# Attention backward on one core: how head rows lie in DRAM, and who turns the dS tiles

## The chip, the cores and the metric

The kernel runs on one core of a Trainium2 chip. A core has five engines that run their own instruction streams and meet through semaphores: TensorE (PE, matrix products; PEld is its weight load), VectorE (DVE), ScalarE (ACT), GpSimd (POOL) and SyncE (SP), which here does nothing but issue DMAs. ScalarE and GpSimd issue some DMAs too. SBUF is the on-chip memory with 128 partitions, PSUM takes the products of TensorE, DRAM lies outside. The metric is device time in microseconds (us), the median of several runs.

## What is computed

The reference is one transformer block with conditional layer norm, its output, and the gradients of nine inputs:

```python
h = _layernorm(x) * (1 + ca) + sa
x = x + ga * _A_ref(h, A_wqkv, A_wo)            # attention, 32 heads of 16, sequence 2048, width 512
h = _layernorm(x) * (1 + cb) + sb
x = x + gb * _B_ref(h, B_w1, B_b1, B_w2, B_b2)  # dense 512 -> 1792, squared relu, 1792 -> 512
...
_out, _vjp = jax.vjp(_f, A_x, A_wqkv, A_wo, B_w1, B_b1, B_w2, B_b2, c, w_mod)
_grads = _vjp(grad_out)
```

The change touches the attention. Forward, for each head: scores = q k^T / 4, p = softmax(scores), o = p v. Backward, with dO the gradient of o: dP = dO v^T, dS = p * (dP - delta), where delta is the row sum of dO * o; then dq = dS k, dk = dS^T q, dv = p^T dO. dS lies with queries on the partitions; dq needs it with keys there, so every tile of dS has to be turned (transposed).

## The kernel before

The program has five parts in time: preparation (layer norm, the first products, to about 42 us), the forward attention with the dense parts of three of the four query chunks woven in (42 to 1006), the last dense chunk (1006 to 1124), the attention backward (1124 to 2390), and the remaining gradients (2390 to 2514).

**Head rows.** A matmul of one head contracts over 16 rows, and TensorE's tiles have 32. Four heads make a group of 128 rows, HG = 8 groups: head h of a group has partitions 32h to 32h+31. Rows 0 to 15 of these are its data (q, k, v or dO, turned so that the sequence runs along the row). Row 16 holds one side of a bound or correction: ones for k and v, the row's negative bound on the score (`m_st`) for q, and -delta (`d_st`) for dO; thereby one product gives score minus bound, or dP minus delta. The other 15 rows are zeros (q, dO) or ones (k, v), which contribute nothing. In DRAM only the data rows are kept (`qkT_st`, `vT_st`, `dOT_st`), with `m_st` and `d_st` beside them. `row_loads` (L131) loads a group tile as four DMAs of 16 rows, one for each head, and a fifth for the bound's rows; the spare rows were filled once, by memsets (L979, L980, `head_fill` L1201, L1505, L1506) and by `copy_const` on ScalarE (L1232).

**Forward.** Units of 128 keys run through (query chunk, group, key tile). `fload` (L544) loads a group's k and q through SyncE, 16 units ahead, into two buffers each: nine DMAs. A unit has four score products (L560), two exponentials of ScalarE over 128x1024 (`ET`, L562), and four products with v (L576).

**Backward.** The loop goes through 512 units: group hg, key chunk kc (512 keys), query chunk qc, query tile qi; four units with the same chunks are a batch, and there are 128 batches. In a unit:
- `score` (L1595): four products, one for each head, 128 queries x 512 keys, into one of three PSUM banks; `expo` (L1601): four exponentials on ScalarE into E_u (four buffers).
- `dp_pair` (L1615): two products into psD_u (two buffers), and one VectorE product dS_u = psD_u * E_u over 128x1024 (L1617); twice a unit. Two units share one dS_u tile; there are four such tiles.
- `k_quad` (L1655) and `v_quad` (L1664): products for dk and dv.
- `transpose_unit` (L1624 on): after each second unit SyncE issues one DMA that turns both units' dS (1 MB, L1632) into dsT (three buffers, one a batch).
- `dq_quad` (L1682): two batches later, products of dsT with k into the dq accumulator; `dq_out` copies them out on ScalarE (L1695) and adds on GpSimd (L1700).

In odd batches (`on_pe`, L1620) the last unit is turned otherwise: unit 2 alone by a DMA of 0.5 MB (L1630), unit 3 by 16 transposes on TensorE (`pe_turn`, L1645) with two copies out of PSUM on ScalarE (L1761). TensorE's order of work within a batch is written out by hand as a string of tokens: s a score, e an exponential, D a dp_pair, q a quad, t a turn on TensorE, T its copy, d half of dq's products, Q their way out, f a filler matmul that keeps TensorE busy. `order_t` holds the turns and four fillers, `order_n` neither:

```python
toks, bank = order_t if on_pe(b - 1) else order_n
```

Between batches, ScalarE's queue issues the next group's loads (`plan_head`, L1579, through `load`, L1577): four loads of q in its other layout, 4 + 5 + 4 + 5 of k, q, v and dO, one every four D tokens. It also stores the results of dk and dv four times a group (a quarter each, L1667 on) and those of dq four times a group.

**Queues.** Every DMA issued by SyncE stands in one queue in program order; an instruction there that waits or takes long holds up the ones behind it. The order of all engines in these parts is the program's.

Of the kernel before, what the change touches and what calls it, by code (L numbers as in the profile page):

```python
# [17 lines left out]
BF = dt.bfloat16  # L18
# [16 lines left out]
def kernel(  # L35
# [55 lines left out]
    qkT_st = dram.tile([2, D, n], BF, name="qkT_st")  # L91
    vT_st = dram.tile([D, n], BF, name="vT_st")
    dOT_st = dram.tile([D, n], BF, name="dOT_st")
    m_st = dram.tile([H, n], BF, name="m_st")
    d_st = dram.tile([H, n], BF, name="d_st")
# [35 lines left out]
    def row_loads(dst, srcT, hg, cols, aux=None):  # L131
        for h in range(4):
            i = hg * 4 + h
            yield dst[32 * h:32 * h + DH, :], srcT[i * DH:(i + 1) * DH, cols]
        if aux is not None:
            yield dst.rearrange("(h c) n -> c h n", h=4)[DH], aux[hg * 4:(hg + 1) * 4, cols]

    def load_rows(*args):
        for to, fro in row_loads(*args):
            SP.dma_start(out=to, in_=fro)  # L140
# [6 lines left out]
    with ExitStack() as ph:  # L147
# [385 lines left out]
        def store_grad(c, lag, dOT, dlt, more=3):  # L533
            dltT = wk.tile([P, P], BF, name="dltT", tag="dltT", bufs=1)
            later(lag, sp, dltT[:], dlt.rearrange("p t h -> p (t h)"), True)
            cols = slice(512 * c, 512 * c + 512)
            later(lag + more, sp, dOT_st.rearrange("(b p) n -> p b n", p=P)[:, :, cols], dOT.rearrange("p b t q -> p b (t q)"))
            for ti in range(4):
                later(lag + more, sp, d_st[:, 512 * c + ti * P:512 * c + (ti + 1) * P], dltT[H * ti:H * ti + H, :])
# [4 lines left out]
        def fload(qc, hg):  # L544
            i = hg % 2
            kt_sb, qt_sb = kts[i], qts[i]
            load_rows(kt_sb, qkT_st[1], hg, slice(0, n))
            load_rows(qt_sb, qkT_st[0], hg, slice(512 * qc, 512 * qc + 512), m_st)
            fh[qc, hg] = (qt_sb, kt_sb)
# [115 lines left out]
        def later_stage(i):  # L665
            if i < 4:
                vT = tmpT[:, 4 * (i % 2):4 * (i % 2) + 4, :].rearrange("p a q -> p (a q)")
                sp(vT[:, 0:n], v_st[:, i * P:(i + 1) * P], True)
                later(3, sp, vT_st[i * P:(i + 1) * P, :], vT[:, 0:n])
                return  # L670
# [79 lines left out]
        qkT_v = qkT_st.rearrange("a (b p) n -> p a b n", p=P)  # L750
# [64 lines left out]
        def value_tile(t, acc):  # L815
            for ic in range(DC):
                PE.matmul(acc, h1Ts[t // 4][:, ic, (t % 4) * P:(t % 4 + 1) * P], wqkv[:, ic, 2 * D:3 * D],
                          start=(ic == 0), stop=(ic == DC - 1))
            if t % 4 == 0:
                psp["v"] = cb.tile([P, 4, D], BF, name="vP", tag=("a_c", "xn2_c")[t // 4 % 2])  # L820
            vt = psp["v"][:, t % 4, :]
            DVE.tensor_copy(vt, acc)
            DVE.tensor_copy(vaug[:, t, 0:H, 0:DH], vt.rearrange("p (h d) -> p h d", d=DH))
            if t % 4 == 3:
                later(1, sp, v_st.rearrange("(t p) d -> p t d", p=P)[:, t - 3:t + 1, :], psp["v"][:])
# [10 lines left out]
        def mod_rows(j):  # L836
            pm = mm()
            for ic in range(DC):
                PE.matmul(pm[:], sbcT[:, ic, :], wmod_slice(j)[:, ic, :], start=(ic == 0), stop=(ic == DC - 1))
            if j in (1, 4):  # L840
                DVE.tensor_scalar(modbc[:, j, :], pm[:], 1.0, None, ALU.add)
            else:
                DVE.tensor_copy(modbc[:, j, :], pm[:])

        def prep():
# [28 lines left out]
            DVE.tensor_reduce(onecol, identb.rearrange("p (h c) -> p c h", c=32)[:, DH, :], AX.X, ALU.add)  # L874
            POOL.memset(sel0, 0.0)
# [84 lines left out]
            sp(qkT_st[1, 0:P, :], KTs[0][:])  # L960
            sp(qkT_st[0, 0:P, 0:512], sP[:, 4, :])
# [13 lines left out]
            for k in range(2):  # L975
                sp(m_st[4 * k:4 * k + 4, 0:512], mrow.rearrange("(h c) n -> c h n", h=4)[DH + k])
            for t in range(4):
                value_tile(t, acc4()[:])
            POOL.memset(kts[1][:], 1.0)  # L979
            POOL.memset(qts[1][:], 0.0)  # L980
# [3 lines left out]
            run_due(True)  # L984
# [3 lines left out]
        def plan_tasks():  # L988
# [5 lines left out]
            def key_tile(b, g):  # L994
# [8 lines left out]
                if g == QC - 1:  # L1003
                    later(1, sp, qkT_st[1, b * P:(b + 1) * P, :], KTs[b][:])
# [6 lines left out]
            def query_tile(g, hb):  # L1011
# [7 lines left out]
                if g == 0:  # L1019
                    later(1, sp, qkT_st[0, hb * P:(hb + 1) * P, 0:512], sP[:, lo + hb, :])  # L1020
                elif hb == 3:
                    later(1, sp, qkT_v[:, 0, :, chunk_cols(g)], sP[:, lo:lo + 4, :])
# [10 lines left out]
            def bound(g, hbs):  # L1033
# [10 lines left out]
                later(1, sp, m_st[h0:h1, chunk_cols(g)], mrow[h0:h1, :])  # L1044
# [156 lines left out]
        def head_fill(i):  # L1201
            for key in ("k", "v", "q", "do"):
                POOL.memset(hsets[i][key][:], 1.0 if key in ("k", "v") else 0.0)

        def kvq_loads(hg):
            hs = hsets[hg % 2]
            for i in range(4):
                yield hs["qs"][:, 4 * i:4 * i + 4, :], q_st[hg][:, 4 * i:4 * i + 4, :]
            yield from row_loads(hs["k"], qkT_st[1], hg, slice(0, n))
            yield from row_loads(hs["q"], qkT_st[0], hg, slice(0, n), m_st)  # L1210
            yield from row_loads(hs["v"], vT_st, hg, slice(0, n))
# [22 lines left out]
        def last_chunk(O_c, L, w1T, w2T):  # L1234
# [76 lines left out]
            later(17, copy_const, hsets[0]["v"][:], 1.0)  # L1311
# [109 lines left out]
            def grad(ti):  # L1421
                attn_grad(c, ti, daT, woT, dOs_c, O_c, dlt)
                ACT.activation(dpad[:, ti, :, 0:DH], dOs_c[:, ti, 0:4 * DH].rearrange("p (h d) -> p h d", d=DH), AF.Identity)
                ACT.activation(dpad[:, ti, :, DH:DH + 1], dlt[:, ti, 0:4].unsqueeze(2), AF.Identity)
# [69 lines left out]
        with ExitStack() as ph2:  # L1494
            pools["mm"] = ph2.enter_context(tc.tile_pool(name="psM2", bufs=4, space=bass.MemoryType.PSUM))
            with tc.manual_schedule(engines={PE.engine, ACT.engine, DVE.engine, SP.engine, POOL.engine}):
# [8 lines left out]
                DVE.memset(hsets[0]["q"][:], 0.0)  # L1505
                DVE.memset(hsets[0]["do"][:], 0.0)  # L1506
                copy_const(hsets[0]["k"][:], 1.0)
# [17 lines left out]
                def head_loads():  # L1525
                    done = slice(0, 512 * (QC - 1))
                    for i, (to, fro) in enumerate(list(kvq_loads(0)) + list(row_loads(hsets[0]["do"][:, done], dOT_st, 0, done, d_st))):
                        later(i, sp, to, fro)
# [20 lines left out]
    with ExitStack() as ph:  # L1549
# [29 lines left out]
        def plan_head(hg):  # L1579
            j0 = (hg - 1) * 128 + 14  # L1580
            loads = list(kvq_loads(hg)) + list(row_loads(hsets[hg % 2]["do"], dOT_st, hg, slice(0, n), d_st))
            for i, (to, fro) in enumerate(loads):
                at(j0 + 4 * i, load, to, fro)
# [37 lines left out]
        def on_pe(b):  # L1621
            return b % 2 == 1
# [35 lines left out]
        def v_quad(u):  # L1658
# [7 lines left out]
            if qt == TT - 1:  # L1666
# [3 lines left out]
                else:  # L1670
                    part = slice(kc * 512, (kc + 1) * 512)
                    at(cur["j"] + 4, load, dVKtP[hg][:, part], hst[hg]["vk"][:, part])
# [12 lines left out]
        def dq_out(b):  # L1685
# [15 lines left out]
            if kc == QC - 1 and qc == QC - 1 and hg < HG - 1:  # L1701
                for hq in range(4):
                    r = hg % 2 * 64 + hq * DH
                    at(cur["j"] + 6 + hq, load, dQc[hg // 2, r:r + DH, :], st["dq"][32 * hq:32 * hq + DH, :])
# [16 lines left out]
        with tc.manual_schedule(engines={PE.engine, ACT.engine, DVE.engine, SP.engine, POOL.engine}):  # L1721
            head_fill(1)
# [329 lines left out]
```

## Time and profile before

| what | us |
|---|---|
| runs: median (all) | 2519.93 (2519.93, 2520.61, 2513.72) |
| profiled execution: span from first to last instruction | 2513.8 |
| busy: TensorE, ScalarE, VectorE, GpSimd | 2335.0, 2302.6, 1809.7, 348.0 |
| 41 to 1006: busy TensorE, ScalarE, VectorE (of 965) | 862.1, 942.4, 454.2 |
| 1006 to 1124: the same (of 118) | 111.9, 53.3, 79.6 |
| 1124 to 2390: the same (of 1266) | 1212.4, 1228.4, 1186.2 |
| 2390 to 2514: the same (of 124) | 117.5, 50.3, 62.3 |
| mean granted TensorE clock, whole span | 0.982 |

The profiled execution took as long as the fastest of the three runs, so sums that start from its span are compared with runs that spread by 7 us (0.3%). Rows of a group give the busy time of all its instructions, the mean duration of one in ns, and the idle time of the engine just before them with what ended most of it. Durations of consecutive instructions overlap on ScalarE and VectorE, so start to start is shorter than the mean duration. SyncE has no busy row: its instructions only issue, and appear as SPq with a start and a duration.

### The profile page before, as it was taken

To read this page: it belongs to the slowest core of one execution; us is meant where nothing else is said; L and a number is where in the kernel's file an instruction comes from. 1 tells how busy PE (TensorE), PEld (TensorE's weight loads), DVE (VectorE), ACT (ScalarE), POOL (GpSimd) and SP (SyncE) were. 2 spreads that over 40 slices of the span, in tenths; PEclk is the share of its full clock that TensorE was granted. 3 is DMA by queue.
4 is the path that set the end of the run, shared out by engine and by line. 5 is a ranking of instruction groups with operands and counts; after the bars stand their busy time and mean duration, and the time that the engine had idled before them with its cause. 6 is when DMAs were issued, how large, how long until landed. Compare 5 with 4: busy or idle time off the path is not lost.

```text
span 2513.8 us, 49777 instructions
## 1 busy us (share of the span) xinstructions
PE 2335.0 (93%) x18916; PEld 777.9 (31%) x19005; DVE 1809.7 (72%) x2317; ACT 2302.6 (92%) x3577; POOL 348.0 (14%) x370
## 2 busy tenths in 40 slices
PE   7898889989988998999999999999999999999999
PEld 3232223222322323442233322233222323222343
DVE  6555153455435454579999999999998999999872
ACT  7999999999999999539999999999999999999952
POOL 2000000210333142210111101011010110110100
PEclk9999999999999999999999999999999999999999
DMA  6476465356748765969999999999999999999972
GB/s 203 129 193 177 136 131 139 96 160 136 110 88 174 153 131 118 264 211 184 207 203 210 199 198 204 204 201 206 204 200 206 199 195 204 206 199 215 197 254 72
DMA packets 1220981, 447.15 MB, mean 178 GB/s; under 512 B 1096951, under 2 KB 1191607, under 8 KB 1220486
## 3 DMA queue, kind: packets, MB, share of 16 engines
q1 hardware_dynamic: 1192822, 409.11, 81.8%
q0 software_dynamic: 10944, 16.78, 4.5%
q10 hardware_dynamic: 16976, 18.07, 2.8%
q8 instruction: 149, 2.44, 0.4%
q14 instruction: 90, 0.74, 0.1%
HBM read 96.75 MB, written 73.95 MB: 68 GB/s over the span
## 4 chain that ended last, share of the span: by engine, by line
PE 40%; ACT 39%; issue 7%; DVE 7%; DMA 4%; SPq 2%; ACTq 1%; POOL 0%; DVEq 0%; another core or an unknown queue 0%
ACT E_u L1601 24%; ACT ET L562 11%; PE dqacc L1682 5%; PE psST L560 4%; PE psS_A L1595 3%; PE pm L233 3%; PE accVK L1655 2%; ACT dsT L1761 2%; PE oacc L576 2%; PE psS_B L1595 2%; SPq L178 2%; PE psS_C L1595 2%; PE pm L412 2%; PE pdh L1876 2%; PE pwq L1910 2%
## 5 line engine op out<-in xcount | busy, mean ns | idle before, releaser
L1617 DVE TENSOR_TENSOR dS_u<-psD_u,E_u 128x1024 bf16<-128x1024 f32 x1024 | 1186.2, 1219 | 71.2 <-PE psD_u L1615 25.5
L562 ACT ACTIVATE ET<-psST 128x1024 bf16<-128x1024 f32 x1024 | 942.3, 1247 | 25.3 <-PE psST L560 24.7
L1601 ACT ACTIVATE E_u<-psS_A 128x512 bf16<-128x512 f32 x768 | 509.6, 664 | 11.0 <-PE psS_C L1595 8.5
L1601 ACT ACTIVATE E_u<-psS_B 128x512 bf16<-128x512 f32 x768 | 502.6, 654 | 12.5 <-PE psD_u L1615 3.4
L1615 PE MATMUL psD_u<-iv,ido 32*128 32x512 bf16 x2048 | 409.9, 388 | 0.5 <-DVE dS_u L1617 0.2
L560 PE MATMUL psST<-qt_sb,kt_sb 32*128 32x512 bf16 x2048 | 316.5, 387 | 53.0 <-ACT ET L562 46.2
L1601 ACT ACTIVATE E_u<-psS_C 128x512 bf16<-128x512 f32 x512 | 333.7, 652 | 2.7 <-PE psS_B L1595 1.0
L1595 PE MATMUL psS_B<-ik,iq 32*128 32x512 bf16 x768 | 294.9, 384 | 12.5 <-ACT E_u L1601 5.0
L1595 PE MATMUL psS_A<-ik,iq 32*128 32x512 bf16 x768 | 293.4, 382 | 11.1 <-DVE dwlast L237 1.0
L1595 PEld LDWEIGHTS <-iq 32*128 32x128 bf16 x2048 | 130.5, 91 | 316.0 <-issue 299.9
L1655 PE MATMUL accVK<-dS_u,qz 128*32 128x512 bf16 x2048 | 213.0, 390 | 0.5 <-PE psD_u L1615 0.3
L576 PE MATMUL oacc<-ET,vaug 128*32 128x512 bf16 x2048 | 207.8, 396 | 1.9 <-DVE ostage L580 1.9
L1664 PE MATMUL accVK<-E_u,dOs_tok 128*16 128x512 bf16 x2048 | 203.7, 386 | 0.0
L1700 POOL TENSOR_TENSOR dQacc<-dQacc,dqtmp 128x512 f32<-128x512 f32 x64 | 81.3, 1271 | 851.4 <-ACT dqtmp L1695 851.4
L1595 PE MATMUL psS_C<-ik,iq 32*128 32x512 bf16 x512 | 194.6, 380 | 4.2
L560 PEld LDWEIGHTS <-kt_sb 32*128 32x128 bf16 x2048 | 85.4, 91 | 341.0 <-issue 320.4
L1682 PE MATMUL dqacc<-dsT,KS_tok 128*32 128x512 bf16 x2048 | 147.7, 387 | 18.7 <-DMA dsT<-dS_u 4.3
L1761 ACT ACTIVATE dsT<-ptT 128x1024 bf16<-128x1024 bf16 x128 | 145.3, 1135 | 7.0 <-PE ptT L1645 6.4
L251 DVE COPY part<-pm 128x512 f32<-128x512 f32 (+2 forms) x103 | 63.5, 617 | 117.5 <-PE pm L233 106.0
L1615 PEld LDWEIGHTS <-ido 32*128 32x128 bf16 x2048 | 105.0, 91 | 100.7 <-issue 94.5
L1655 PEld LDWEIGHTS <-qz 128*32 128x32 bf16 x2048 | 58.5, 94 | 177.8 <-issue 162.8
L576 PEld LDWEIGHTS <-vaug 128*32 128x32 bf16 x2048 | 53.0, 93 | 121.0 <-issue 121.0
(407 smaller groups left out, 2499.5 us busy)
## 6 DMA issues: line engine op xcount, KB each, us to landing
p_st<-part POOLq DMA_DIRECT2D x36, 256.0 KB, 5.2
kt_sb<-qkT_st SPq DMA_DIRECT2D x124, 64.0 KB
wA<-in_B_w_dram SPq DMA_DIRECT2D x28, 256.0 KB
wB<-w1T_st SPq DMA_DIRECT2D x21, 256.0 KB
wA<-w2T_st SPq DMA_DIRECT2D x21, 256.0 KB
wB<-in_B_w_dram SPq DMA_DIRECT2D x21, 256.0 KB
p_st<-part POOLq DMA_DIRECT2D x25, 192.0 KB, 4.2
p_st<-part SPq DMA_DIRECT2D x18, 256.0 KB
```

What stands on the lines that cost most here:

```text
L560: PE.matmul(ps[:, hi, :], kt_sb[r:r + 32, kt * P:(kt + 1) * P], qt_sb[r:r + 32, :], start=True, stop=True, tile_position=(r, 0))
L562: ACT.activation(ET[:, 2 * pair:2 * pair + 2, :], ps[:], AF.Exp, scale=SCALE)
L576: PE.matmul(oacc[32 * hq:32 * hq + 32, :], lhsT, ET[:, hq, :], start=(kt == 0), stop=(kt == TT - 1), tile_position=(0, 32 * hq), skip_grou ...
L1595: PE.matmul(psS[:], st["q"][r:r + 32, qt * P:(qt + 1) * P], st["k"][r:r + 32, kc * 512:kc * 512 + 512], start=True, stop=True, tile_positi ...
L1601: ACT.activation(bst[u][0][:, hq, :], sst.pop((u, hq))[:], AF.Exp, scale=SCALE)
L1615: PE.matmul(psD[:, hi, :], st["do"][r:r + 32, qt * P:(qt + 1) * P], st["v"][r:r + 32, kc * 512:kc * 512 + 512], start=True, stop=True, til ...
L1617: DVE.tensor_tensor(dS_u[:, 2 * pair:2 * pair + 2, :], psD[:], E_u[:, 2 * pair:2 * pair + 2, :], ALU.mult)
L1655: PE.matmul(cur["vk"][32 * hq:32 * hq + 32, :], hst[hg]["qz"][:, qt, hq, :], bst[u][1][:, hq, :], start=(qt == 0), stop=False, tile_positi ...
L1664: PE.matmul(acc[32 * hq:32 * hq + DH, :], dOs_tok[:, qt, (hg * 4 + hq) * DH:(hg * 4 + hq + 1) * DH], E_u[:, hq, :], start=False, stop=(qt ...
L1682: PE.matmul(acc[32 * hq:32 * hq + 32, :], KS_tok[:, kc * 4 + kt, h * DH:h * DH + 32], tT[:, :, hq * 4 + kt, :], start=(kt == 0), stop=(kt ...
L1700: POOL.tensor_tensor(dst2, dst, tmp[:], ALU.add)
L1761: ACT.activation(dst, pt[:], AF.Identity)
```

## The change

Three things change.

- *DRAM layout.* `qkT_st`, `vT_st`, `dOT_st`, `m_st` and `d_st` become four arrays qP, kP, vP, oP of 1024 rows, 32 for each head, data on the even rows and spare rows between; the bound's row is the first spare row (row 1 of a head). Spare rows are filled once by 16 DMAs of 512 KB (`spare_fill`) from two constant tiles. The fills of SBUF tiles by VectorE, ScalarE and GpSimd go.
- *Loads.* A group tile is one contiguous DMA of 128 rows. A forward group has two loads instead of nine; a backward group five instead of 22, one every twelve D tokens; dk and dv are stored once a group instead of four times.
- *Turning.* `on_pe` is always false: every batch has two turning DMAs of 1 MB, none of 0.5 MB, no transposes of dS on TensorE, and always the order `order_n`.

```diff
-    qkT_st = dram.tile([2, D, n], BF, name="qkT_st")
-    vT_st = dram.tile([D, n], BF, name="vT_st")
-    dOT_st = dram.tile([D, n], BF, name="dOT_st")
-    m_st = dram.tile([H, n], BF, name="m_st")
-    d_st = dram.tile([H, n], BF, name="d_st")
+    qP, kP, vP, oP = (dram.tile([2 * D, n], BF, name=f"{x}P_st") for x in "qkvo")
...
+    def data_rows(x):
+        return x.rearrange("(i two) n -> two i n", two=2)[0]
+
+    def spare_rows(x):
+        return x.rearrange("(i two) n -> two i n", two=2)[1]
+
+    def bound_rows(x):
+        return x.rearrange("(h c) n -> c h n", c=2 * DH)[1]
+
+    def group(x, hg, cols=slice(0, n)):
+        return x[hg * P:(hg + 1) * P, cols]
...
-            load_rows(kt_sb, qkT_st[1], hg, slice(0, n))
-            load_rows(qt_sb, qkT_st[0], hg, slice(512 * qc, 512 * qc + 512), m_st)
+            sp(kt_sb[:], group(kP, hg))
+            sp(qt_sb[:], group(qP, hg, slice(512 * qc, 512 * qc + 512)))
...
+        def spare_fill(x, b, src):
+            sp(spare_rows(x)[b * P:(b + 1) * P, :].rearrange("p (a n) -> p a n", a=2), src.unsqueeze(1).to_broadcast([P, 2, 1024]))
...
+            for k in range(2):
+                plain[k] = flat(cb.tile([P, 3, 4, P], BF, name="plain", tag="tk", bufs=5)[:, 0:2].rearrange("p f t q -> p (f t) q"))
+                POOL.memset(plain[k], float(k))
...
+            spare_fill(kP, 0, plain[1])
+            spare_fill(qP, 0, plain[0])
...
-            POOL.memset(kts[1][:], 1.0)
-            POOL.memset(qts[1][:], 0.0)
+            for b in range(1, 4):
+                later(1 + b, spare_fill, kP, b, plain[1])
+                later(2 + 2 * b, spare_fill, qP, b, plain[0])
+            for b in range(4):
+                later(40 + 4 * b, spare_fill, vP, b, plain[1])
+                later(42 + 4 * b, spare_fill, oP, b, plain[0])
...
-            for i in range(4):
-                yield hs["qs"][:, 4 * i:4 * i + 4, :], q_st[hg][:, 4 * i:4 * i + 4, :]
-            yield from row_loads(hs["k"], qkT_st[1], hg, slice(0, n))
-            yield from row_loads(hs["q"], qkT_st[0], hg, slice(0, n), m_st)
-            yield from row_loads(hs["v"], vT_st, hg, slice(0, n))
+            yield hs["qs"][:], q_st[hg]
+            for key, x in (("k", kP), ("q", qP), ("v", vP)):
+                yield hs[key][:], group(x, hg)
...
-            later(17, copy_const, hsets[0]["v"][:], 1.0)
...
-                DVE.memset(hsets[0]["q"][:], 0.0)
-                DVE.memset(hsets[0]["do"][:], 0.0)
-                copy_const(hsets[0]["k"][:], 1.0)
...
-            loads = list(kvq_loads(hg)) + list(row_loads(hsets[hg % 2]["do"], dOT_st, hg, slice(0, n), d_st))
-            for i, (to, fro) in enumerate(loads):
-                at(j0 + 4 * i, load, to, fro)
+            for i, (to, fro) in enumerate([*kvq_loads(hg), (hsets[hg % 2]["do"][:], group(oP, hg))]):
+                at(j0 + 12 * i, load, to, fro)
...
         def on_pe(b):
-            return b % 2 == 1
+            return False
...
-                else:
-                    part = slice(kc * 512, (kc + 1) * 512)
-                    at(cur["j"] + 4, load, dVKtP[hg][:, part], hst[hg]["vk"][:, part])
+                elif kc == QC - 1:
+                    at(cur["j"] + 2, load, dVKtP[hg], hst[hg]["vk"][:])
...
-            head_fill(1)
```

The stores of q, k, v, dO, the bounds and delta go to `data_rows` and `bound_rows` of the new arrays with the same bytes; the last dense chunk writes its dO tile on even rows; the dq stores keep their number and come a little earlier.

## The prediction

> **What bounds the kernel now.** I read the page's groups first, then the rows of the tile that the change is about, then the order of time on SyncE and VectorE in the middle of the backward loop.
>
> ```profile
> span 2513.8 us, 49777 instructions
> L1617 DVE TENSOR_TENSOR dS_u<-psD_u,E_u 128x1024 bf16<-128x1024 f32 x1024 | 1186.2, 1219 | 71.2 <-PE psD_u L1615 25.5
> L1682 PE MATMUL dqacc<-dsT,KS_tok 128*32 128x512 bf16 x2048 | 147.7, 387 | 18.7 <-DMA dsT<-dS_u 4.3
> L1761 ACT ACTIVATE dsT<-ptT 128x1024 bf16<-128x1024 bf16 x128 | 145.3, 1135 | 7.0 <-PE ptT L1645 6.4
> ```
>
> By the page ScalarE and VectorE share the backward loop: the busy windows give 1228 us of ScalarE and 1186 us of VectorE in the 1266 us from 1124 to 2390. TensorE waited for a turned tile for 4.3 us only. From this the turning DMAs look free. They are not, which the next view shows.
>
> ```profile
> L1632 SPq DMA_TRANSPOSE dsT<-dS_u x192: 4752/5312/7226, 1132.3 to 2377.9; - x192
> L1630 SPq DMA_TRANSPOSE dsT<-dS_u x64: 1724/2770/4503, 1149.3 to 2382.8; - x64
> ```
>
> These are the durations on SyncE's queue (min/median/max in ns) of the turning DMAs: 192 of 1 MB (L1632) and 64 of 0.5 MB (L1630). 192 x 5.312 + 64 x 2.770 = 1197.2 us. The first starts at 1132.3 and the last ends at 2382.8 + 3.3 = 2386.1: a stretch of 1253.8 us. SyncE is inside one of these instructions for 95% of the loop.
>
> ```profile
> 1498.02 5.59 SPq L1632 DMA_TRANSPOSE dsT<-dS_u  x1
> 1503.70 2.11 SPq L1630 DMA_TRANSPOSE dsT<-dS_u  x1
> 1505.98 16.63 SPq L1632 DMA_TRANSPOSE dsT<-dS_u  x3
> 1523.00 3.01 SPq L1630 DMA_TRANSPOSE dsT<-dS_u  x1
> ...
> 1485.57 11.47 DVE L1617 TENSOR_TENSOR dS_u<-psD_u,E_u 128x1024 bf16<-128x1024 f32 x10 [0.37 <-PE psD_u L1615]
> 1497.27 7.23 DVE L1617 TENSOR_TENSOR dS_u<-psD_u,E_u 128x1024 bf16<-128x1024 f32 x6 [0.24 <-PE psS_A L1595]
> ```
>
> The reader should see that one starts 0.09 us after the other ends (1498.02 + 5.59 = 1503.61, next start 1503.70). The question is whether a long row is work or a wait for the data. The DMA at 1503.70 turns the third unit of its batch, whose last VectorE product ended at 1495.90 (inside the run of ten above, counted in the trace): the data lay ready for 7.8 us, and what held the DMA was the one before it. So SyncE works them off one by one, and its idle time is 1253.8 - 1197.2 - 256 x 0.09 = 33.6 us. The list of waits says otherwise, 939.6 us of SyncE on dS_u at L1632; but VectorE ticks the same semaphore every 1.13 us, and the list takes the last tick before an instruction's end for what released it. Starts and ends decide here.
>
> **The change, part by part.**
>
> *No turning on TensorE.* Every second batch loses its 16 transposes (1024 in all, some 0.62 us for eight), its two copies on ScalarE (L1761, 128 x 1135 ns, 145.3 us busy) and the fillers of the order with turning. Batches that begin under the order without turning already take 8.54 us, those under the other one 10.8 (starts of every sixteenth E_u). If nothing else held the loop, VectorE would: ten products in 11.47 us are (11.47 - 1.22)/9 = 1.139 each, 8 x 1.139 = 9.11 us a batch, 1166 us for 128 batches against 1255.6 now (1125.7 to 2381.3). The most this part can be worth is 89 us. I take zero of it, because of the next part.
>
> *64 DMAs grow from 0.5 MB to 1 MB.* SyncE now has 256 instructions of the 1 MB kind: 256 x (5.312 + 0.09) = 1382.9 us against the stretch of 1253.8. The same by differences: 64 x (5.312 - 2.770) = 162.7, of which 33.6 fit the present idle time. **+129.1 us**. It can't be hidden, as SyncE is one queue and the whole loop feeds it. What is late next: dS_u has four buffers of two units, so VectorE's next product waits until the DMA four tiles back has landed; then the two psD_u banks stay full, TensorE stops at that product's matmuls, and the scores queued behind them (L1595) keep ScalarE's exponentials waiting. dq's matmuls (L1682) stop at dsT as well. All go at SyncE's pace, 2 x 5.40 = 10.80 us a batch, and ScalarE's saved 145 us turns into idle time.
>
> The price of a 1 MB row is the term to bound. Packet records show 32 of the 192 with nothing else on any DMA queue: mean 5.00. With ScalarE's loads beside them 71 rows have 5.11, with instruction fetches alone 36 rows 5.47, with both 53 rows 5.77. The loads and fetches stay, so 5.00 is not reached; the third 1 MB row in succession has a mean of 5.21, the one just after a 0.5 MB row 5.44. I bound by 5.10 and 5.44: 256 x 5.19 = 1328.6 (+74.8) and 256 x 5.53 = 1415.7 (+161.9), and take the median of all, since the new rows have the same neighbours as the old in about the same mix.
>
> The Trainium skill speaks against this. "Advanced Engine Details and Errata", section "X-Bar Transpose (TRN2)", has transposing DMAs as fast as plain ones, at an expected 350 to 400 GB/s; that would make 1 MB an estimated 2.6 to 3.0 us, SyncE would be half idle, and the loop would fall to VectorE's pace, the first rival below. The row differs: 1.049 MB in 5.312 us is 197 GB/s, and 0.524 MB in 2.770 us is 189 GB/s. The measurement decides.
>
> *Loads of the backward loop.* ScalarE's queue issues 206 DMAs at L1577 now; 154 loads become 35, 24 stores of vk become 6, the 28 of dq stay: 137 fewer at 0.31 to 0.50 us, some 45 us of ScalarE, covered since ScalarE waits for SyncE anyway. Without that cover it would be worth up to 45. But each head's k, q, v and do are 512 KB instead of 256, so 7 MB more pass beside the turning DMAs. The rows with and without loads differ by 0.11 us, at most 256 x 0.11 = 28 us if every one were hit harder; against it TensorE has 7% fewer instructions to fetch. Net zero, both inside the bounds above.
>
> *Forward attention.* Nine loads for a head group become two (8 x about 0.4 + 0.55 us of SyncE become some 0.9). ScalarE is the bound there (942 us busy of 965), and the group issued from 60.8 to 65.7 is needed at 73.9, so nothing is gained; the doubled k load (512 KB) lands in the same 8 us. Zero. Were it late, the first groups would wait a few us each.
>
> *Filling the spare rows.* Sixteen stores of 512 KB, about 0.45 us of SyncE each. Eight stand before the first group's loads, and the first bound rows wait until a fill has landed; but SyncE is idle from 51.4 to 59.8 there, waiting for values to store, which takes in 8 x 0.45 and a landing. Zero, at worst 3 us. The other eight come 40 units later, when SyncE has room. POOL gives up fills of 1.80 and 0.53 us for two of half that size.
>
> *Between the phases.* VectorE's fills of q and do (2 x 0.91 us, in the chain of waits at 1009.1 to 1011.1) and ScalarE's of k and v (2 x 1.9) go. Up to 2.0 us; TensorE's own matmuls of L641 run to 1011.42 right behind, so I take 0.3.
>
> *The end.* The last DMA is 1 MB instead of 0.5; its issue is in the sum, and from SyncE's last end to the landing it is the same 2 to 3 us. The dq and vk loads behind it on SyncE's queue move with it.
>
> **Sum**: 2513.8 + 129.1 - 0.3 = 2642.6 for an execution like the profiled one, which is the lowest of the three (2513.72). The median is 6 above it, so 2643 to 2649; I say **2645**. With the bounds: 2588 to 2676, and 6 more for the median.
>
> **Rivals.**
>
> *The long rows are pace, not work.* If SyncE's instruction stretches only because its tiles come no faster, the DMAs would speed up with the loop, and VectorE would set the end: 2513.8 - 89 = 2425. For it: the list of waits, and 0.5 MB rows as short as 1.72. Against: 1 MB rows never go below 4.75, also when the data lay ready for 4 us. Chance 0.04.
>
> *The shortest row becomes the usual one* (no half-size DMAs between): 256 x (4.752 + 0.09) = 1239.6, a batch 9.68 us, above VectorE's 9.11: 2513.8 - 14.2 = about 2500. Against: rows in succession have 5.2 to 5.4. Chance 0.03. Any price under 4.81 is faster than now.
>
> *TensorE's clock as well.* TensorE now pauses about 10.80 - 8.54 = 2.3 us in each batch, and the fillers that closed its pauses are gone. At 1128 to 1138 the granted clock was 0.50 for 10.2 us. Half clock for less than 4.6 us of a batch is paid from the pause; for 7 us it costs 3.5 - 2.3 = 1.2 us a batch, 128 x 1.2 = 154 more, some 2800. Against: three tiles queued before SyncE, some 16 us, cover single events. Chance 0.06.
>
> That the change does not do what it says is out: its SyncE order holds 256 turning DMAs at one line, and TensorE's holds none of dS.
>
> **How the numbers follow.** The serial queue at 5.1 to 5.5 us: 0.87. Range 2590 to 2690: the bounds with the run's spread, and a little of the clock's case. Faster by over 0.3% (the least a measurement here can tell) comes from the first two rivals, 0.06; within 0.3% from a price of about 4.84, 0.01; slower 0.93.
>
> **What would show it.** Right: 256 rows of the turning DMA back to back with a median of 5.1 to 5.5; ScalarE's and VectorE's busy digits in the loop down to about eight tenths; VectorE's idle time ended by landings of dsT or, at second hand, by dqacc; a loop of 1380 us with an end section of 124 unchanged. Wrong: rows under 4.8, gaps between SyncE's rows, VectorE still at nine tenths, or a granted clock well under 0.95 in the loop with TensorE busy throughout.

## The result, and the profile after

| | time, us (median, range) | runs | profiled span, us |
|---|---|---|---|
| before | 2520.3 (2513.7 to 2528.3) | 4 | 2513.8 |
| after | 2685.6 (2682.0 to 2690.2) | 4 | 2688.4 |

The ratio is 1.067 (95% interval 1.063 to 1.070): 165 us slower, where 125 were forecast; the time lies just inside the upper end of the range.

The groups of the changed kernel that answer to those shown before (line, engine, operation; busy us and mean ns; idle time of the engine just before and what ended it):

```profile
span 2688.4 us, 46555 instructions
L1619 DVE TENSOR_TENSOR dS_u<-psD_u,E_u 128x1024 bf16<-128x1024 f32 x1024 | 1197.8, 1219 | 225.3 <-PE psD_u L1617 188.2
L1603 ACT ACTIVATE E_u<-psS_B 128x512 bf16<-128x512 f32 x768 | 470.3, 612 | 135.2 <-PE psD_u L1617 127.8
L1683 PE MATMUL dqacc<-dsT,KS_tok 128*32 128x512 bf16 x2048 | 208.7, 494 | 112.8 <-DMA dsT<-dS_u 84.4
```

The work is the same to a per cent (VectorE's products 1186.2 before, 1197.8 now), but VectorE's idle time before it has gone from 71.2 to 225.3 us, and TensorE's wait for a landed dsT from 4.3 to 84.4. The two copies of L1761 are gone; ScalarE got no faster for it.

The rows of the tile dsT and SyncE's order of time in the middle of the loop:

```profile
L1634 SPq DMA_TRANSPOSE dsT<-dS_u x256: 4626/5040/7900, 1134.6 to 2555.0; - x128
```

```profile
1534.76 83.66 SPq L1634 DMA_TRANSPOSE dsT<-dS_u  x15
```

There are 256 turning DMAs of 1 MB, and fifteen of them stand in one unbroken run, 83.66 / 15 = 5.58 us each. Counted over the whole trace they take 1386.2 us, 5.415 in the mean, with 41.0 us between them, in a stretch of 1427.2 us (1253.8 before). When one starts, its data have been ready for 4.5 us in the median, and for more than 1 us in 95% of the cases, and the dsT buffer that it writes has been read out for at least 11.6 us: SyncE waits neither for VectorE nor for a free buffer.

VectorE in the same place:

```profile
1549.77 1.23 DVE L1619 TENSOR_TENSOR dS_u<-psD_u,E_u 128x1024 bf16<-128x1024 f32 x1 [0.28 <-PE psD_u L1617]
1552.48 1.23 DVE L1619 TENSOR_TENSOR dS_u<-psD_u,E_u 128x1024 bf16<-128x1024 f32 x1 [1.48 <-PE psD_u L1617]
1554.44 17.47 DVE L1619 TENSOR_TENSOR dS_u<-psD_u,E_u 128x1024 bf16<-128x1024 f32 x15 [0.74 <-PE psD_u L1617]
1575.43 1.22 DVE L1619 TENSOR_TENSOR dS_u<-psD_u,E_u 128x1024 bf16<-128x1024 f32 x1 [3.52 <-PE psD_u L1617]
```

It works in runs at its own pace (17.47 us for fifteen products) and then stands, up to 3.5 us at a time. The named releaser is TensorE's psD_u, the nearest link; what TensorE waits for itself is dsT, above.

The windows by stage (us of the window; busy time and count of PE, PEld, DVE, ACT, POOL; granted clock, share of the DMA engines, GB/s):

```profile
1128.00:2565.00 1437.00, 1208.38 (x10286) 289.59 (x10283) 1197.81 (x1024) 1145.60 (x2207) 141.37 (x103) 0.82 1.14 206
41.00:1010.00 969.00, 868.53 (x5946) 277.03 (x5946) 450.77 (x882) 942.56 (x1025) 172.22 (x204) 0.98 0.65 158
2565.00:2689.00 124.00, 118.44 (x652) 52.53 (x648) 62.24 (x150) 50.26 (x77) 1.27 (x1) 0.97 0.47 153
```

Nearly all of the loss is in the loop, whose window grew from 1266 to 1437 us. One thing is new there: the granted clock is 0.82 (0.98 before). It asks for a test of its own, since the forecast had a rival with exactly that.

### The profile page after: what moved, and what is told of

It is laid out like the page before. It is cut to its first block, busy times and chain, and to the rows that moved or that the text cites. A ratio compares the mean times of both kernels' runs of the same rounds, so it can differ in the third digit from the quotient of the medians.

```text
span 2688.4 us, 46555 instructions
## 1 busy us (share of the span) xinstructions
PE 2339.2 (87%) x17724; PEld 688.9 (26%) x17724; DVE 1815.3 (68%) x2315; ACT 2216.3 (82%) x3447; POOL 340.0 (13%) x366
## 4 chain that ended last, share of the span: by engine, by line
PE 47%; ACT 22%; DMA 17%; DVE 7%; issue 6%; ACTq 0%; SPq 0%; DVEq 0%; POOL 0%
DMA dsT<-dS_u 15%; ACT E_u L1603 11%; ACT ET L559 10%; PE dqacc L1683 6%; PE psST L557 4%; PE psS_B L1597 4%; PE psS_A L1597 4%; PE accVK L1657 3%; PE psS_C L1597 3%; PE accVK L1666 3%; PE pm L230 3%; PE oacc L573 2%; PE pdh L1876 2%; PE pwq L1910 2%; PE pm L409 2%
## 5 line engine op out<-in xcount | busy, mean ns | idle before, releaser
L1619 DVE TENSOR_TENSOR dS_u<-psD_u,E_u 128x1024 bf16<-128x1024 f32 x1024 | 1197.8, 1219 | 225.3 <-PE psD_u L1617 188.2
L1603 ACT ACTIVATE E_u<-psS_B 128x512 bf16<-128x512 f32 x768 | 470.3, 612 | 135.2 <-PE psD_u L1617 127.8
L1603 ACT ACTIVATE E_u<-psS_C 128x512 bf16<-128x512 f32 x640 | 394.6, 616 | 80.8 <-PE psS_B L1597 62.1
L1617 PE MATMUL psD_u<-iv,ido 32*128 32x512 bf16 x2048 | 459.4, 445 | 1.7 <-DVE dS_u L1619 1.6
L1603 ACT ACTIVATE E_u<-psS_A 128x512 bf16<-128x512 f32 x640 | 395.5, 618 | 37.0 <-PE psD_u L1617 20.6
L1597 PE MATMUL psS_B<-ik,iq 32*128 32x512 bf16 x768 | 341.8, 445 | 13.3 <-ACT E_u L1603 2.3
L1597 PE MATMUL psS_C<-ik,iq 32*128 32x512 bf16 x640 | 269.7, 421 | 95.5 <-ACT E_u L1603 94.6
L1683 PE MATMUL dqacc<-dsT,KS_tok 128*32 128x512 bf16 x2048 | 208.7, 494 | 112.8 <-DMA dsT<-dS_u 84.4
L1657 PE MATMUL accVK<-dS_u,qz 128*32 128x512 bf16 x2048 | 240.4, 457 | 1.4 <-DVE dS_u L1619 0.9
L1683 PEld LDWEIGHTS <-KS_tok 128*32 128x32 bf16 x2048 | 39.9, 100 | 234.2 <-issue 192.2
L1666 PEld LDWEIGHTS <-dOs_tok 128*16 128x16 bf16 x2048 | 49.7, 87 | 150.2 <-issue 150.2
```

Source lines behind the costliest of these rows:

```text
L1597: PE.matmul(psS[:], st["q"][r:r + 32, qt * P:(qt + 1) * P], st["k"][r:r + 32, kc * 512:kc * 512 + 512], start=True, stop=True, tile_positi ...
L1603: ACT.activation(bst[u][0][:, hq, :], sst.pop((u, hq))[:], AF.Exp, scale=SCALE)
L1617: PE.matmul(psD[:, hi, :], st["do"][r:r + 32, qt * P:(qt + 1) * P], st["v"][r:r + 32, kc * 512:kc * 512 + 512], start=True, stop=True, til ...
L1619: DVE.tensor_tensor(dS_u[:, 2 * pair:2 * pair + 2, :], psD[:], E_u[:, 2 * pair:2 * pair + 2, :], ALU.mult)
L1657: PE.matmul(cur["vk"][32 * hq:32 * hq + 32, :], hst[hg]["qz"][:, qt, hq, :], bst[u][1][:, hq, :], start=(qt == 0), stop=False, tile_positi ...
L1666: PE.matmul(acc[32 * hq:32 * hq + DH, :], dOs_tok[:, qt, (hg * 4 + hq) * DH:(hg * 4 + hq + 1) * DH], E_u[:, hq, :], start=False, stop=(qt ...
```

## The experiments

Theory: SyncE's queue of turning DMAs is serial and full, so that the loop lasts as long as its 256 rows. Rivals: the order without turns on TensorE is slower by itself, through its pauses or through the low clock; the new layout of the head rows costs what is put down to the turns; or one big DMA is dearer than two small ones.

| run | loop, us | mean turning row | clock in the loop | median, us | ratio to before (95%) |
|---|---|---|---|---|---|
| before | 1254.7 | 5.343 (1 MB) | 0.98 | 2520.3 | |
| after | 1421.1 | 5.415 | 0.82 | 2685.6 | 1.0669 (1.0634 to 1.0704) |
| e1_layout | 1275.2 | 5.502 (1 MB) | 0.98 | 2548.9 | 1.0105 (1.0069 to 1.0141) |
| e2_turns | 1393.2 | 5.289 | 0.83 | 2659.1 | 1.0549 (1.0516 to 1.0581) |
| e3_half | 1450.0 | 2.714 (0.5 MB) | 0.82 | 2726.1 | 1.0814 (1.0783 to 1.0845) |
| e4_warm | 1417.1 | 5.416 | 0.96 | 2690.6 | 1.0675 (1.0624 to 1.0726) |
| e5_half_turns | 1283.6 | 5.064 (128) | 0.88 | 2551.9 | 1.0121 (1.0091 to 1.0150) |
| e6_noloads | 1369.4 | 5.232 | 0.82 | 2644.8 | 1.0498 (1.0480 to 1.0516) |
| e7_noloads_old | 1365.2 | 5.202 | 0.84 | 2636.1 | 1.0464 (1.0443 to 1.0485) |
| e8_split | 1427.0 | 5.448 | 0.83 | 2699.9 | 1.0712 (1.0688 to 1.0737) |
| e9_half_warm | 1222.1 | 5.276 (128) | 0.99 | 2492.9 | 0.9899 (0.9876 to 0.9921) |
| e10_pool_loads | 1274.5 | 5.484 (1 MB) | 0.97 | 2530.5 | 1.0057 (1.0034 to 1.0080) |
| e11_merged | 1277.7 | 5.353 (1 MB) | 0.97 | 2538.9 | 1.0073 (1.0049 to 1.0097) |
| e12_before_warm | 1251.2 | 5.283 (1 MB) | 1.00 | 2517.9 | 1.0009 (0.9995 to 1.0022) |

The loop is from the first to the last of ScalarE's E_u in the profiled execution; rows and clock are of that execution too. The medians are of four or more runs, e4_warm's of two. Each ratio is to runs of before made beside that run; their medians lie between 2515.7 and 2521.5 us, so a difference of two rows here carries up to 6 us of that.

**The two halves of the change apart.** e1_layout has the new layout and loads with the old share of turns on TensorE; e2_turns has the old layout and loads with all turns by DMA.

```diff
# e1_layout, against after
-            return False
+            return b % 2 == 1
# e2_turns, against before
-            return b % 2 == 1
+            return False
```

> The changed kernel with odd batches turned on TensorE again: the new DRAM layout and loads alone. Theory (SyncE works the turning DMAs off one by one, and the 64 DMAs that grew from 0.5 to 1 MB are the cost): the time goes back to near the kernel before, 2520 to 2550 us, with SyncE's stretch of turning DMAs near 1254 to 1280 us; the rest over before is the 512 KB head loads, beside which a 1 MB row took 6.4 us in the changed kernel against 5.1 beside the small loads. Rival (the layout with its double bytes is what costs): above 2620 us.

> The kernel before with no turn on TensorE: the other part of the change alone, with the old small loads. Theory: nearly all of the loss, 2640 to 2685 us, SyncE's stretch 256 rows x (5.2 to 5.4 + 0.1) = 1360 to 1410 us with no idle time left. Rival (layout): below 2560 us.

The rows of dsT, of e1_layout (again 192 large and 64 small ones) and then of e2_turns (256 large ones):

```profile
L1634 SPq DMA_TRANSPOSE dsT<-dS_u x192: 4827/5328/9628, 1143.7 to 2411.9; - x192
L1632 SPq DMA_TRANSPOSE dsT<-dS_u x64: 1814/2903/5610, 1160.7 to 2416.8; - x64
```

```profile
L1632 SPq DMA_TRANSPOSE dsT<-dS_u x256: 4702/5206/8442, 1130.2 to 2524.1; - x128
```

The turns alone cost 2659.1 - 2520.3 = 139 us, and the layout alone 2548.9 - 2520.3 = 29. Their sum, 168, is the whole change (165). So the turns are five sixths of it, and the layout is not free.

**One large DMA or two small ones.** e3_half turns each unit as soon as it is done, in 512 DMAs of 0.5 MB.

```diff
...
-            elif qi % 2 == 1:
-                SP.dma_start(out=dqt[u // 4][:, qi - 1:qi + 1]..., in_=cur["dS"]..., transpose=True)
+            SP.dma_start(out=dqt[u // 4][:, qi], in_=bst[u][1].rearrange("p h k -> p (h k)"), transpose=True)
```

> The changed kernel, each unit turned by a DMA of its own: 512 of 0.5 MB instead of 256 of 1 MB, the same bytes. If the DMA engines' rate for turned bytes is the limit: 2.45 to 2.7 us a row, the same 10.8 us a batch, 2660 to 2700 us. If it is the 1 MB instruction that is slow (in the kernel before, 0.5 MB rows with nothing beside them took 1.84 us, 1 MB rows 5.0): about 1.9 to 2.2 us a row, 4 x 2.1 = 8.4 us a batch, and VectorE's 9.1 us a batch sets the loop: 2430 to 2480 us, below the kernel before.

```profile
L1630 SPq DMA_TRANSPOSE dsT<-dS_u x512: 1722/2516/6422, 1136.3 to 2595.6; - x171
```

The shortest row, 1722 ns, does not last: in a row of their own the small DMAs take 2.714 us in the mean, 512 x 2.714 = 1389.6 us, which is what 256 large ones take (1386.2). The turned bytes have a price, not the count of DMAs; the gaps after twice as many (71.6 against 41.0 us) make up the other 30 us of the loop.

**The clock.** e4_warm adds seven filler matmuls a batch to the order without turns.

```diff
-            "s0 D s1 q e0 q s2 e1 e2 D s3 s4 q s5 e3 D e4 "
+            "s0 D s1 q e0 q s2 e1 e2 D f s3 s4 q s5 e3 D f e4 "
...
```

> The changed kernel with seven filler matmuls a batch in TensorE's order, so that its pauses are filled and the granted clock (0.82 in the loop of the changed kernel) stays up. Theory (SyncE's queue bounds, the half clock is hidden behind the tiles queued there): 2675 to 2700 us whatever the clock does. Rival (the clock is a good part of the loss): clock above 0.95 in the loop and 2560 to 2640 us.

The busy windows of after and of e4_warm over the same stretch of the loop:

```profile
1140.00:2370.00 1230.00, 1036.05 (x8833) 247.01 (x8829) 1033.56 (x885) 987.57 (x1905) 121.83 (x88) 0.82 1.14 206
```

```profile
1140.00:2370.00 1230.00, 1077.73 (x9610) 301.75 (x9609) 1032.73 (x886) 993.17 (x1905) 121.77 (x88) 0.96 1.14 206
```

The clock rises from 0.82 to 0.96, and VectorE does as many products in the 1230 us as before (885 and 886): no gain. In after, the batches that run at a clock of 0.95 or more take 9.38 us in the mean (62 of 128) and those between 0.6 and 0.8 take 13.4 (30). It looks as if the clock set the pace. In e4_warm 105 batches run at 0.95 or more, and these take 10.42. SyncE's queue holds the mean; the clock only shares it out. My reading is that the tiles that lie ready before SyncE level it: in e4_warm a turning DMA's data have been ready for 5.5 us in the median when it starts.

**Is SyncE all that holds it?** e5_half_turns halves the turning DMAs, e9_half_warm adds four fillers to that.

```diff
# e5_half_turns, against after
-            elif qi % 2 == 1:
+            elif qi == 1:
-  ... tT[:, :, hq * 4 + kt, :],
+  ... tT[:, 0:2, hq * 4 + kt, :].unsqueeze(1).to_broadcast([P, 2, 2, P]),
# e9_half_warm, against e5_half_turns
-  ... e6 e7 d1 e8 ...  e14 e15 D q
+  ... e6 e7 f f d1 e8 ...  e14 e15 D q f f
```

> The changed kernel, but only the first two of each batch's four units are turned (128 DMAs of 1 MB in place of 256), and dq's matmuls read these two units twice, so that TensorE does as much work as before and dq comes out of the wrong data. Theory (SyncE's serial queue of turning DMAs is all that holds the loop): SyncE needs 128 x 5.5 = 704 us and is idle half the time; the loop falls to VectorE's pace, 8 x 1.14 = 9.1 to 9.3 us a batch against 11.1, some 1170 to 1190 us for 128 batches against 1427, and the time to 2430 to 2460. Rival (the order without turns on TensorE, its pauses or its clock hold the loop as well): the batch stays above 10 us and the time above 2540. A time between the two, about 2500, would say that another engine stands close behind SyncE.

> The kernel with half the turns, and four filler matmuls a batch where TensorE pauses in its order (two ahead of dq's matmuls, two ahead of the next batch's scores). Without fillers 92 of its 128 batches ran at a granted clock of 0.95 or more and took 9.28 us in the mean, the 36 others 10.9 to 12.4 at 0.5 to 0.95. Theory (TensorE's clock is the second limit behind SyncE: once SyncE has room, batches at half clock are too long for TensorE): the loop's clock rises from 0.88 to 0.95 or more, and most of 36 batches x 2.7 = 96 us comes back: 2460 to 2490. Rival (the long batches come from something else and the low clock follows from their pauses): the clock rises, the time stays above 2535.

The clock in fortieths of the span (tenths of full speed) and the wait of dq's matmuls in e5_half_turns:

```profile
PEclk9999999999999999997889899889888999888899
```

```profile
L1683 PE MATMUL dqacc<-dsT,KS_tok 128*32 128x512 bf16 x2048 | 184.4, 442 | 25.5 <-ACT E_u L1603 16.3
```

No wait for a landed dsT is left, and 134 us come back, which shows that the queue held the loop. But I had expected 225 to 255. The loop stays 96 us above 128 batches at the pace of the 92 that run at full clock (128 x 9.28 = 1188 against 1283.6), and at 0.88 VectorE does not reach its own pace. With the fillers:

```profile
PEclk9999999999999999998999999999999999999999
```

```profile
1140.00:2370.00 1230.00, 1159.58 (x10895) 323.50 (x10895) 1185.99 (x1035) 1126.12 (x2207) 140.70 (x103) 0.99 0.70 132
```

The clock is 0.99, VectorE is busy 1186 of 1230 us, and another 59 us are gone (2551.9 to 2492.9; 2460 to 2490 were expected), or 53 when each is held against the runs of before beside it (30 above, 23 below). Here the clock does cost time. So two limits lie one behind the other in the changed kernel: SyncE's queue, and, hidden by it, a TensorE that pauses and then runs at half clock. Of the 96 us of the loop some 60 came back (1283.6 to 1222.1); the fillers cost TensorE something themselves, as a batch at full clock takes 9.48 us with them and 9.28 without.

**What the layout costs.** e6_noloads and e7_noloads_old leave out the loads of the heads 2 to 7, in after and in e2_turns; e8_split cuts after's loads in four.

```diff
# e6_noloads, against after; e7_noloads_old, against e2_turns
-            plan_head(hg)
+            if hg == 1:
+                plan_head(hg)
+            else:
+                at((hg - 1) * 128 + 54, spread_qz, hg)
# e8_split, against after
-                at(j0 + 12 * i, load, to, fro)
+                for r in range(4):
+                    at(j0 + 16 * i + 4 * r, load, to[32 * r:32 * r + 32], fro[32 * r:32 * r + 32])
```

> The changed kernel without the loads of the heads 2 to 7 in the backward loop (six of seven heads; they compute with the data of heads 0 and 1). Theory (loads of 512 KB beside the turning DMAs lengthen these: 28 rows with a load alone have a mean of 6.41 us and 22 with a load and a fetch 6.86, against 4.92 and 5.42 without): 6/7 of 28 x 1.49 + 22 x 1.44 = 63 us less, 2610 to 2635, and the mean row falls from 5.42 to 5.15 to 5.2. Rival (the rows beside loads are long for another reason, or time lost there is made up later): within 15 of 2686.

> The kernel before with all turns by DMA (its old loads of 256 KB for each tile, in 22 pieces a head), without the loads of the heads 2 to 7. By the rows of that kernel with its loads, 83 with a load alone at 5.15 and 65 with both at 5.71 against 4.95 and 5.38 without, the loads cost 17 + 21 = 38 us, six sevenths of it 33: 2615 to 2635 from 2659. If the 27 us between this layout and the new one with all turns by DMA (2659 and 2686) are the loads of the loop alone, the two kernels without loads come within 5 of each other; if part of it stands in the forward phases (its profile begins the loop 4 to 5 us later), the new layout stays that much above.

> The changed kernel with each head's loads of the loop in four pieces of 32 rows, four VectorE products apart, in place of one DMA of 128 rows every 12 products; the bytes are the same. Theory A (the bytes beside the turning DMAs cost): within 8 of 2686. Theory B (a 512 KB burst costs more than the same bytes spread out, as 6.41 against 5.15 us of a row suggests): 10 to 30 less, 2655 to 2676, and rows with a load beside them fall toward 5.3.

Without loads the new layout gains 2685.6 - 2644.8 = 41 us and the old one 2659.1 - 2636.1 = 23; both gains are some two thirds of what the rows with and without loads had made me expect (63 and 33). Per byte they agree, as far as differences that are uncertain by some us can tell. A head's loads are 4 x 0.5 + 0.25 = 2.25 MB in the new layout and 4 x 0.25 + 0.25 = 1.25 MB in the old one, so six heads cost 41 / 13.5 = 3.0 us per MB and 23 / 7.5 = 3.1. The padding is paid with time on the turning queue, about 18 us by these times and 24 by the loops of the table, though TensorE, ScalarE and VectorE never wait for a load there.

The rest, 2644.8 - 2636.1 = 9 us, comes for the most part not from the loop (1369.4 and 1365.2 us in the profiles) but from what lies ahead of it: the loop begins at 1134.2 instead of 1126.3. From the first to the last ET of the forward attention the eight profiles with the new layout take 968.7 to 977.5 us, the six with the old one 962.8 to 967.2. Compared group by group (32 ET each, seven new against three old), the first group is 7.9 us longer and the fourth 6.0; two later ones give 3.6 and 2.1 back. ScalarE's first exponentials, before and after (the last bracket is the idle time ahead and its releaser):

```profile
41.71 11.11 ACT L562 ACTIVATE ET<-psST 128x1024 bf16<-128x1024 f32 x12 [3.46 <-PE psST L560]
55.79 24.87 ACT L562 ACTIVATE ET<-psST 128x1024 bf16<-128x1024 f32 x27 [2.98 <-PE psST L560]
```

```profile
41.07 11.11 ACT L559 ACTIVATE ET<-psST 128x1024 bf16<-128x1024 f32 x12 [3.46 <-PE psST L557]
60.48 1.94 ACT L559 ACTIVATE ET<-psST 128x1024 bf16<-128x1024 f32 x2 [8.30 <-PE psST L557]
63.36 17.52 ACT L559 ACTIVATE ET<-psST 128x1024 bf16<-128x1024 f32 x19 [0.94 <-PE psST L557]
```

The pause after twelve exponentials grows from 2.98 to 8.30 us. What waited for what in after between 50 and 61 us (us in total, times, longest):

```profile
DVE vP L819 <- DMA v_st<-vP: 8.7, 1, 8.7
ACT ET L559 <- PE psST L557: 8.3, 1, 8.3
PE pm L814 <- DVE vP L819: 7.8, 1, 7.8
```

and SyncE's order of time:

```profile
45.67 1.50 SPq L175 DMA_DIRECT2D kP_st<-plain  x1
47.21 0.50 SPq L175 DMA_DIRECT2D qP_st<-plain  x1
47.76 0.87 SPq L175 DMA_DIRECT2D kP_st<-plain  x1
48.67 1.21 SPq L175 DMA_DIRECT2D qP_st<-plain  x1
52.40 1.14 SPq L175 DMA_DIRECT2D qP_st<-sP  x2
53.65 0.36 SPq L175 DMA_DIRECT2D rows_st<-racc  x1
54.11 0.40 SPq L175 DMA_DIRECT2D v_st<-vP  x1
```

and before:

```profile
47.45 0.42 SPq L178 DMA_DIRECT2D rows_st<-racc  x1
47.92 1.59 SPq L178 DMA_DIRECT2D v_st<-vP  x2
```

Read it from the end: the exponential waits for scores, these stand on TensorE behind a product that waits for VectorE's vP, and this buffer comes free when the store v_st has landed. That store is issued at 54.11 (before: 47.92, and VectorE's wait there was 2.9). Ahead of it stand four fills, and SyncE's own 2.4 us from 49.88 to 52.40, put down to the landing of a fill of qP that the bound rows are written over. In the fourth group kt_sb is issued at 166.43 instead of 152.61, with six fills of vP and oP in the 32 us ahead of it on SyncE; that these set its time is read from the order. No run leaves out the fills alone, so both places are read from waits and order, and not shown by an experiment.

e8_split lies outside both forecasts: the same bytes in 20 pieces a head take 2699.9, 14 us more than in 5. Spreading a burst does not help. A row beside a load does get shorter (5.50 us against 6.41, and 6.21 against 6.86 with a fetch too), but 116 rows instead of 50 now have one, and together they lie 80 us above rows without a load, against 73 in after. That is near theory A. In the profiles 6 of the 14 us stand in the loop and 4.5 ahead of it, where the two kernels are the same, so the price of the pieces themselves stays open.

**Towards a version that beats both.** Three changes to the kernel before: its loads on POOL's queue, fewer and larger loads, and fillers for its order without turns.

```diff
# e10_pool_loads, against before
-            ACT.dma_start(out=to, in_=fro)
+            POOL.dma_start(out=to, in_=fro)
# e11_merged, against before
-            for i in range(4):
-                yield hs["qs"][:, 4 * i:4 * i + 4, :], q_st[hg][:, 4 * i:4 * i + 4, :]
+            yield hs["qs"][:], q_st[hg]
...
-                else:
-                    part = slice(kc * 512, (kc + 1) * 512)
-                    at(cur["j"] + 4, load, dVKtP[hg][:, part], hst[hg]["vk"][:, part])
+                elif kc == QC - 1:
+                    at(cur["j"] + 2, load, dVKtP[hg], hst[hg]["vk"][:])
# e12_before_warm, against before
-            ... s14 s15 e14 e15 D q
+            ... s14 s15 e14 e15 D q f f
```

> The kernel before, with the 206 loads and stores of the backward loop issued on POOL's queue in place of ScalarE's; the same bytes in the same pieces. If ScalarE's issues (0.31 to 0.50 us each, some 80 us) stand on the path that sets the loop's end, as ScalarE is busy 1225 of 1262 us there, up to 33 us are to be had before SyncE's queue, idle for 33.6 us, is full: 2485 to 2510. If SyncE's queue already sets the end, within 8 of 2521. A slower time would say that POOL's way of issuing costs the transfers more.

> The kernel before, with two merges of the change that do not alter any bytes: a head's token rows of q in one load in place of four, and the store of a head's dK and dV once in place of four times (39 issues fewer on ScalarE's queue in the loop). 39 x 0.4 = 16 us of ScalarE: 2505 to 2518 if ScalarE sets the pace, within 6 of 2521 if SyncE's queue does; 5 to 10 more if larger transfers in one piece cost the turning DMAs more than small ones.

> The kernel before, with two filler matmuls at the end of each batch that runs under the order without turns (which had none). Theory (the clock costs the kernel before a little too: in its profile 9 of 128 batches ran below a granted clock of 0.95 and took 11.7 us in the mean against 9.65, 9 x 2.05 = 18 us): 2500 to 2513, faster than both kernels. Rival (SyncE's queue sets its pace over the whole loop and a low clock only fills pauses, or the fillers take as much of TensorE as they save): within 8 of 2520.

None does. e10_pool_loads is 15 us slower than the runs of before beside it: on POOL's queue the same loads make the 1 MB rows 5.484 us instead of 5.343, and SyncE's rows sum to 1234.1 us instead of 1194.8. Whether ScalarE's issues hold the loop before is not settled by it, since the time between SyncE's rows fell from 59.0 to 39.2 us while the rows themselves grew by more. e12_before_warm brings the loop's clock to 1.00 and changes nothing (1.0009). Either the clock of 0.98 had cost nothing, or the fillers take what they save: batches at full clock last 9.75 us with them and 9.65 without, 13 us over 128 batches against the 18 that were hoped for. The rival named both, and the run doesn't part them. e11_merged is 23 us slower than the runs of before beside it (2515.7), where 2 to 10 faster, or 5 to 10 slower, were expected. Its rows are no longer than before's (5.353), but more time lies between them (75.8 against 59.0 us), and 17 batches instead of 9 run below a clock of 0.95. Why is open: it merges a load and a store at once, and e8_split shows splitting to be slower as well.

## Why the prediction was right, and where its sizes were off

The mechanism held: the serial queue became the end of the loop. Step by step, in the profiled executions:

- **64 DMAs grow from 0.5 to 1 MB (+129.1).** This is the term that carried the forecast, and it came near. e2_turns measures this step with "No turning on TensorE" at +139, inside the bounds of +74.8 to +161.9. In the profile of after the stretch is 1427.2 instead of 1382.9. Of these 44 us, 26 are the row: 256 x (5.415 - 5.312). A median was used for a skewed distribution; with before's own mean of 5.343 the step would have had 8 of them, and the other 18, 256 x (5.415 - 5.343), fit the price of the loads. The remaining 18 are gaps, 41.0 where 256 x 0.09 = 23 was taken. The queue was treated as never empty, and it did stand a little. That 5.312 came so near the mean is partly luck: the median, by which the row was priced and which was to show it (5.1 to 5.5), fell to 5.040, under the lower bound of 5.10. What made up for it are the 50 rows beside 512 KB loads, at 6.41 and 6.86 us, which the term did not contain.
- **No turning on TensorE (zero).** Right in this kernel, as the time was SyncE's. Its ceiling of 89 us rested on VectorE being next; e5_half_turns and e9_half_warm show that TensorE at its low clock is.
- **Loads of the backward loop (net zero, at most 28).** This is the step that failed, by size. The doubled bytes cost some 18 us in the loop (24 by the profiles), through the turning DMAs. The bound from the rows (28) held; the offset against it, fewer instructions to fetch, was an argument without a row, and did not come: 42% of the rows have a fetch beside them in after, 46% of the 1 MB rows before, and beside a fetch alone they take 5.42 and 5.47 us.
- **Filling the spare rows (zero, at worst 3), forward attention (zero).** Also too small: 4.5 us in the profiled execution (968.7 against 964.2), 8 to 13 in the other profiles. The prediction counted eight issues and a landing against an idle 8.4 us on SyncE, but not the store of v that they push back on that queue, and who waits for that.
- **Between the phases (-0.3).** From the last ET to the first E_u it is 118.5 us in after, 118.6 before.
- **The end.** From SyncE's last turning row to the end 126.6 us, 127.7 before.

Together: 173.4 in the stretch (forecast 129.1), +2.3 ahead of it and -1.0 behind it make the 174.6 us between the two profiled executions. The sum's own bounds end at 2676, or 2682 with the 6 us for the median. The measured 2685.6 lies above them, and inside the range only by what was added for the runs' spread and the clock; by e4_warm the clock cost nothing here. That the number fell inside is in so far luck.

The rivals. "Pace, not work" is out: the data lay ready, and the rows stay at 5.06 us in the mean when the loop runs faster and the queue is idle half the time (e5_half_turns). "The shortest row" is out by the mean of 5.4, where 4.75 was needed. "TensorE's clock as well" is half true. The clock fell to 0.82, lower than its own sign in the forecast, but TensorE was not busy throughout, and e4_warm shows that it cost nothing at SyncE's pace; its price of 154 us was for a loop that no queue levels. In e5_half_turns and e9_half_warm, with room on SyncE, the clock's price was 53 to 59 us.

## What to carry to other kernels

A queue that is inside its instructions for 95% of a loop is the loop's bound in waiting, also where no list of waits names it: compare starts, ends and the time at which the data were ready. Price a change to its rows by their mean among the transfers they will have as neighbours, and count bytes on other queues as its work too. When a bound is lifted, look for the one behind it before crediting the whole difference: the granted clock was at 0.82 and harmless until SyncE had room.

## What was not expected of the hardware

- A turning DMA from SBUF to SBUF keeps to about 4.86 us for 1 MB even with a queue that is idle half the time (median of 128 in e5_half_turns, 1.049 MB / 4.862 us = 216 GB/s, by the duration of the instruction). With half the turned bytes in flight it gained 3.5% on the 5.040 of after. The 350 to 400 GB/s of the Trainium skill ("Advanced Engine Details and Errata", "X-Bar Transpose (TRN2)") were not seen in any run: the shortest 1 MB row is 4.51 us (e4_warm, 233 GB/s), the shortest of 0.5 MB 1.70 us (e10_pool_loads, 309 GB/s). What sets the 4.86 us, SyncE's instruction or the transfer behind it, no run here parts; e3_half shows only that it goes by the bytes.
- Large loads beside it hurt more than small ones, row by row: 6.41 us beside a 512 KB load (28 rows of after), 5.11 beside smaller ones (71 rows of before), 4.92 and 5.00 alone. Over a whole loop the price was some 3 us per MB, with large loads (41 us for 13.5 MB) as with small ones (23 for 7.5).
- In the changed kernel TensorE's granted clock was at 0.50 for 512 us of the loop, in pieces of mostly 3.4 to 10.2 us. In e5_half_turns no pause of TensorE in the loop was longer than 1.0 us, and they sum to 11% of it, yet 304 us were at 0.50; four filler matmuls a batch were enough for 0.99.
